# The second group's two w_out products as seven block products, and its w_in product ordered by block column

## The chip, the cores and the metric

The kernel runs on one core of one Trainium2 chip. Its time is that of one execution on the device, in microseconds (us); it is compared as the median of several executions.

## The reference

An attention layer that mixes heads before and after the softmax is followed by two feed-forward layers:

```python
scores = scale * np.matmul(q, k.transpose(0, 1, 3, 2))           # 4 batches, 12 heads, 448 x 448, head size 64
scores = np.einsum('bhij,hg->bgij', scores, w_pre)
attn = softmax(scores)                                            # over the last axis
attn = np.einsum('bhij,hg->bgij', attn, w_post)
x = np.matmul(attn, v)                                            # as 1792 tokens x 768
h = x @ w_in;  g = np.maximum(h, 0) ** 2;  x = g @ w_out          # first layer: w_in 768 x 2048, w_out 2048 x 768
h = x @ w_in2; g = h * np.clip(h + 3, 0, 6) / 6; y = g @ w_out2   # second layer, same sizes
```

## The kernel before

The four batches are done in two groups of two. Each group runs attention for its 896 tokens and then the two feed-forward layers. Every float32 matrix product there is made of three products of parts: each operand is split into a high part and a low part (what the high part leaves), and high by high, low by high and high by low are summed in PSUM. TensorE sees 128x128 weight blocks against 448 token columns, so one instruction is a 128x128x448 matmul.

*Attention* (class Attention). A group has 90 tiles of ten query rows by twelve heads. `slot(i)` writes one step of a pipeline over tiles: `fetch` (a transfer t<-s, six tiles ahead, on SyncE's queue, called SP here), `premix` (TensorE, three tiles ahead), `top`, `soft`, `scale` (GpSimd makes w2s for the next tile), `postmix` and `keep`. Fetches of q, k and v, and the score and value products, are placed in slots by `plan`. The tiles t have eight buffers, so SP may run ahead until a buffer is missing. The order on each engine is the order in the program.

*Feed-forward* (class Mlps). The weights come in units of 128 rows by 768 columns: 16 units for w_in (kind "h", one per 128 hidden columns) and 16 for w_out (kind "p") in each layer. The first group reads each as float64 words, converts them and writes a float32 copy to DRAM (`kept`); the second group reads the copies. `split_high` and `split_low` make wh on ScalarE and wl on VectorE or GpSimd, one unit ahead. One unit is 36 matmuls: 3 products x 6 blocks x 2 batches. `hidden` and `project` issue them; `act` and `split_g` make the activation and its two parts.

*The second group* already has one product in another form: the second layer's w_in product (kind "s"). Two units of w_in (256 hidden columns) and the token matrix are cut into 2x2 blocks, and four block results come from seven block products instead of eight (the Winograd form of Strassen's scheme). `prepare`, during the first layer's w_in units, loads two kept units, makes four sums of their blocks on VectorE and writes them to DRAM (`sums`); `finish_mixed` makes the token side from the first layer's output while it leaves PSUM; `product` issues 9 matmuls for one block product; `combine`, `step` and `relu` add the results and form the activation. There are 56 such products, 504 matmuls in place of 576. The last product (w_out of the second layer) is direct.

SP's queue takes all loads and stores in program order, with the waits in front of each; results leave on ScalarE's queue.

Of the kernel before, what the change touches and what calls it, by code (L numbers as in the profile page):

```python
# [44 lines left out]
LATE = 10  # L45
# [20 lines left out]
def attention_mlp_kernel(ctx: ExitStack, tc, qT, kT, v, w_pre, w_post, mask, w1_in, w1_out, w2_in, w2_out, outT):  # L66
# [56 lines left out]
    class Attention:  # L123
# [317 lines left out]
        def run(self, ap, behind):  # L441
# [21 lines left out]
    kept, sums = {}, {}  # L463
    HW = DM // 2

    class Mlps:
        def __init__(self, gi, att):
            self.gi, self.att = gi, att
            self.last = gi > 0 and gi == B // NB - 1
            self.units, at = [], 0  # L470
            for which, (w_in, w_out) in enumerate(((w1_in, w1_out), (w2_in, w2_out))):
                if self.last and which == 1:
                    self.base = at
                    self.prods = [(p, 2 * j + i) for j in range(NF // 4) for p, i in PRODUCTS]
                    self.units += [("s", which, n, None) for n in range(len(self.prods) // 2)]
                else:
                    self.units += [("h", which, n, (w_in[n], at + n)) for n in range(NF)]
                at += NF
                self.units += [("p", which, n, (w_out[n // NU, n % NU], at + n)) for n in range(DG * NU)]
                at += DG * NU  # L480
            self.W = w1_in.shape[-1]
            self.mp, self.own, self.u, self.r, self.gates = None, {}, {}, {}, 0
            self.gate = self.opened = None
            self.lows, self.loads = set(), set()
            self.arena, self.ready, self.late, self.scaled = None, {}, [], set()
# [5 lines left out]
        def wr(self, n):  # L491
            if n in self.own:
                return self.own[n]
            at = 2 * 2 * self.W + self.W * (n % 3)
            return self.arena[:, at:at + self.W]

        def load(self, n):
            if n >= len(self.units) or n in self.loads:
                return
            self.loads.add(n)  # L500
            kind, _, m, src = self.units[n]
            if self.last and n >= NF:
                self.own[n] = self.mp.tile([P, self.W], F32, tag="wr", name=f"wr{n}", bufs=3)
            elif self.arena is None:
                self.arena = sh.tile([P, 7 * self.W], F32, tag="e1", name=f"arena{self.gi}")
            if self.gi == 0:
                nc.sync.dma_start(out=self.raw(n).bitcast(I64), in_=src[0])
            elif kind != "s":
                nc.sync.dma_start(out=self.wr(n), in_=kept[src[1]])
            else:  # L510
                for i in range(2):
                    p, pair = self.prods[2 * m + i]
                    a = self.base + 2 * pair
                    if p in SUMS:
                        of = sums[pair][:, SUMS[p] * HW:(SUMS[p] + 1) * HW]
                    else:
                        of = kept[a + (p == 4)][:, (p > 1) * HW:(1 + (p > 1)) * HW]
                    nc.sync.dma_start(out=self.wr(n)[:, i * HW:(i + 1) * HW], in_=of)

# [26 lines left out]

        def split(self, n):
            self.split_high(n)
            self.split_low(n)

        def split_high(self, n):
            if n >= len(self.units) or n in self.ready:
                return
            if self.last and n >= self.base and (n - self.base) % 3 == 1:
                both = self.mp.tile([P, 2, self.W], F32R, tag="pr", name=f"wb{n}", bufs=1)
                wh, wl = both[:, 0, :], both[:, 1, :]
            else:
                wh = sh.tile([P, self.W], F32R, tag="wh", name=f"wh{self.gi}_{n}", bufs=2)
                wl = sh.tile([P, self.W], F32R, tag="wl", name=f"wl{self.gi}_{n}", bufs=2)
            nc.scalar.activation(wh, self.wr(n), AF.Copy)  # L560
            self.ready[n] = wh, wl

        def split_low(self, n):
            if n >= len(self.units) or n in self.lows:
                return
            self.lows.add(n)
            wh, wl = self.ready[n]
            eng = nc.vector if self.gi == 0 or self.last and n >= self.base else nc.gpsimd
            eng.tensor_tensor(out=wl, in0=self.wr(n), in1=f(wh), op=ALU.subtract)  # L569
# [34 lines left out]
        def hidden(self, which, fc, e, wh, wl):  # L604
            cols = slice(e * S, (e + 1) * S)
            hp = self.bank("bm", f"ps_h{self.gi}_{which}_{fc}_{e}")
# [39 lines left out]
        def bank(self, tag, name):  # L646
            if self.last:
                return self.mb.tile([128, 512], F32, tag="pb", name=name, bufs=8)
            return bank(tag, name)

        def prepare(self, n):

            if not self.last or n >= NF:
                return
            m, odd = n // 2, n % 2
            if not odd:
                self.pr = self.mp.tile([P, 4, HW], F32, tag="pr", name=f"pr{m}", bufs=1)
                for i in range(2):
                    nc.sync.dma_start(
                        out=self.pr[:, 2 * i:2 * i + 2, :].rearrange("p c f -> p (c f)"), in_=kept[self.base + 2 * m + i])  # L660
                return
            a11, a12, a21, a22 = (self.pr[:, i, :] for i in range(4))
            nc.vector.tensor_tensor(out=a22, in0=a21, in1=a22, op=ALU.add)
            nc.vector.tensor_tensor(out=a21, in0=a11, in1=a21, op=ALU.subtract)
            nc.vector.tensor_tensor(out=a11, in0=a22, in1=a11, op=ALU.subtract)
            nc.vector.tensor_tensor(out=a12, in0=a12, in1=a11, op=ALU.subtract)
            sums[m] = dr.tile([P, 4 * HW], F32, name=f"sums{m}")
            nc.sync.dma_start(out=sums[m], in_=self.pr.rearrange("p c f -> p (c f)"))

        def part(self, hi, lo, src):  # L670
            nc.scalar.activation(hi, src, AF.Copy)
            nc.gpsimd.tensor_tensor(out=lo, in0=src, in1=f(hi), op=ALU.subtract)

        def finish_mixed(self, dg, e, acc):

            def held(tag, name, bufs=2):
                return (sh if bufs > 1 else self.mp).tile([P, S], F32, tag=tag, name=name, bufs=bufs)
            if dg == 0 and e == 0:
                self.b1, self.b2, self.b3 = (
                    sh.tile([P, 4, DB, S], F32R, tag=tag, name=f"b{k}") for k, tag in ((1, "x1"), (2, "x2"), (3, "e1")))  # L680
                self.t1 = [held(("w0", "w0", "w1")[d], f"t1_{d}") for d in range(DB)]
                self.t3 = [held(("w1", "kr", "kr")[d], f"t3_{d}") for d in range(DB)]
            if dg == 1 and e == 0:
                self.t4 = [held(("gh9_0", "gh9_1", "gl9_0")[d], f"t4_{d}", 1) for d in range(DB)]
                self.b4 = [[self.mp.tile([P, S], F32R, tag=f"gh{10 + (j * DB + d) // 2}_{(j * DB + d) % 2}",
                                         name=f"b4_{j}_{d}", bufs=1) for d in range(DB)] for j in range(2)]
            for d in range(DB):
                a = acc[d, e][:, :S]
                b1, b2, b3 = (t[:, :, d, :] for t in (self.b1, self.b2, self.b3))
                t1, t3 = self.t1[d], self.t3[d]  # L690
                if dg == 0 and e == 0:
                    nc.scalar.activation(b1[:, 0], a, AF.Copy)
                    nc.vector.tensor_tensor(out=b1[:, 1], in0=a, in1=f(b1[:, 0]), op=ALU.subtract)
                    nc.scalar.activation(t1, a, AF.Copy)
                elif dg == 0:
                    nc.vector.tensor_tensor(out=t1, in0=a, in1=t1, op=ALU.subtract)
                    nc.scalar.activation(t3, a, AF.Copy)
                    self.part(b2[:, 0], b2[:, 1], t1)
                elif e == 0:
                    nc.scalar.activation(b1[:, 2], a, AF.Copy)  # L700
# [279 lines left out]
```

## Time and profile before

| | |
|---|---|
| median of 3 runs (lowest to highest) | 1394.34 us (1394.15 to 1394.59) |
| the profiled execution: its own time, its span | 1396.4 us, 1394.6 us |
| TensorE matmul (PE) busy | 1373.3 us, 98% of the span |
| VectorE (DVE) busy | 788.9 us, 57% |
| ScalarE (ACT) busy | 568.2 us, 41% |
| GpSimd (POOL) busy | 349.1 us, 25% |
| 16 DMA engines, mean | 129 GB/s |

The profile is of one execution. "Busy" counts an engine's compute instructions, not its waits. A matmul's duration in it (some 365 ns) is the time through the engine's pipeline; the distance from one to the next is read from long chains. Queries of the trace cut the span by stage, list an engine's instructions in order, or follow the chain of work that ended last.

### The profile page before, as it was taken

To read this page: it belongs to the slowest core of one execution; us is meant where nothing else is said; L and a number is where in the kernel's file an instruction comes from. 1 tells how busy PE (TensorE), PEld (TensorE's weight loads), DVE (VectorE), ACT (ScalarE), POOL (GpSimd) and SP (SyncE) were. 2 spreads that over 40 slices of the span, in tenths; PEclk is the share of its full clock that TensorE was granted. 3 is DMA by queue.
4 is the path that set the end of the run, shared out by engine and by line. 5 is a ranking of instruction groups with operands and counts; after the bars stand their busy time and mean duration, and the time that the engine had idled before them with its cause. 6 is when DMAs were issued, how large, how long until landed. Compare 5 with 4: busy or idle time off the path is not lost.

```text
span 1394.6 us, 22295 instructions
## 1 busy us (share of the span) xinstructions
PE 1373.3 (98%) x8428; PEld 1183.0 (85%) x8428; DVE 788.9 (57%) x1441; ACT 568.2 (41%) x1060; POOL 349.1 (25%) x411
## 2 busy tenths in 40 slices
PE   7999999999999999999999999999999999999999
PEld 3677778899989899998987777779999998999998
DVE  4677667877655587765546776763431105875110
ACT  3454434555322355534234544444342214654021
POOL 0222122434200033310012221245663224423000
PEclk9999999999999999999999999999999999999999
DMA  5453533555555455566644535324453112332121
GB/s 164 120 149 97 136 101 102 180 170 163 165 156 162 144 162 170 161 200 187 201 136 129 146 84 147 102 89 137 145 182 99 50 57 69 114 114 91 57 85 40
DMA packets 77585, 179.98 MB, mean 129 GB/s; under 512 B 7846, under 2 KB 51622, under 8 KB 77478
## 3 DMA queue, kind: packets, MB, share of 16 engines
q1 hardware_dynamic: 74021, 173.06, 41.8%
q10 hardware_dynamic: 3456, 5.51, 1.1%
q8 instruction: 66, 1.08, 0.3%
q14 instruction: 42, 0.34, 0.1%
HBM read 103.04 MB, written 36.96 MB: 100 GB/s over the span
## 4 chain that ended last, share of the span: by engine, by line
PE 93%; DVE 3%; DMA 1%; ACT 1%; issue 1%; POOL 0%; SPq 0%; ACTq 0%; POOLq 0%; DVEq 0%
PE ps_h L610 25%; PE ps_a L624 22%; PE ps_o L275 11%; PE ps_m L227 9%; PE ps_w L730 7%; PE bx L624 5%; PE bs L624 5%; PE bx L302 3%; PE bs L302 2%; PE bs L200 2%; PE bx L200 2%; DMA t<-s 1%; PE ps_s L315 1%; DVE wl L569 0%; PE ps_s L200 0%
## 5 line engine op out<-in xcount | busy, mean ns | idle before, releaser
L275 PEld LDWEIGHTS ps_o<-w2s,p 120*112 120x112 f32 (+1 forms) x1440 | 170.5, 178 | 71.4 <-issue 57.1
L244 ACT ACTIVATE p<-ps_m,mx 120x448 f32<-120x448 f32 x180 | 114.0, 633 | 188.5 <-PE ps_o L275 87.5
L275 PE MATMUL ps_o<-w2s,p 120*112 120x120 f32 (+1 forms) x1440 | 182.0, 270 | 1.9 <-POOL w2s L264 1.8
L227 PE MATMUL ps_m<-t,w1f 120*120 120x448 f32 x360 | 167.8, 548 | 7.5 <-DMA t<-s 7.4
L264 POOL TENSOR_SCALAR w2s<-w2f,rz 120x120 f32<-120x120 f32 x180 | 65.8, 365 | 360.8 <-DVE rz L256 317.2
L610 PE MATMUL ps_h<-xh,wh 128*128 128x448 f32 x384 | 140.5, 366 | 1.5 <-DVE xr L310 1.5
L610 PE MATMUL ps_h<-xh,wl 128*128 128x448 f32 x384 | 140.3, 365 | 0.2 <-DVE wl L569 0.2
L610 PE MATMUL ps_h<-xl,wh 128*128 128x448 f32 x384 | 139.6, 364 | 0.1
L290 DVE COPY a<-ps_o 112x480 f32<-112x480 f32 (+1 forms) x176 | 115.0, 653 | 32.0 <-PE ps_o L275 22.2
L602 POOL TENSOR_TENSOR gl<-g,gh 128x448 fp32r<-128x448 f32 x60 | 77.2, 1287 | 219.6 <-ACT gh L601 165.9
L236 DVE TENSOR_REDUCE mx<-ps_m 120x1 f32<-120x448 f32 x180 | 111.5, 620 | 25.2 <-PE ps_m L227 22.1
L569 DVE TENSOR_TENSOR wl<-arena,wh 128x768 fp32r<-128x768 f32 x64 | 62.8, 981 | 104.9 <-ACT wh L560 104.0
L624 PE MATMUL ps_a<-gh,wh 128*128 128x448 f32 x320 | 118.2, 369 | 0.0
L560 ACT ACTIVATE wh<-arena 128x768 fp32r<-128x768 f32 x80 | 67.0, 838 | 123.4 <-PE bs L624 120.4
L624 PE MATMUL ps_a<-gh,wl 128*128 128x448 f32 x320 | 116.5, 364 | 0.0
L560 ACT ACTIVATE wh<-wr 128x768 fp32r<-128x768 f32 x45 | 37.9, 842 | 137.0 <-PE ps_a L624 124.3
L569 DVE TENSOR_TENSOR wl<-wr,wh 128x768 fp32r<-128x768 f32 x29 | 29.7, 1025 | 96.3 <-ACT wh L560 96.3
L587 ACT ACTIVATE r<-ps_h 128x448 f32<-128x448 f32 x64 | 34.8, 543 | 111.4 <-PE ps_h L610 111.4
L610 PEld LDWEIGHTS ps_h<-xh,wh 128*128 128x128 f32 x384 | 72.1, 188 | 7.4 <-issue 1.9
L610 PEld LDWEIGHTS ps_h<-xl,wh 128*128 128x128 f32 x384 | 72.2, 188 | 6.7 <-POOL xl L579 0.9
L599 DVE CAST gh<-g 128x448 fp32r<-128x448 f32 x64 | 39.6, 618 | 66.4 <-ACT g L588 66.4
L610 PEld LDWEIGHTS ps_h<-xh,wl 128*128 128x128 f32 x384 | 72.0, 188 | 5.6 <-DVE wl L569 0.5
(167 smaller groups left out, 3020.7 us busy)
## 6 DMA issues: line engine op xcount, KB each, us to landing
arena<-in_dram SPq DMA_DIRECT2D x64, 768.0 KB
t<-s SPq DMA_DIRECT2D x176, 210.0 KB
keep<-arena SPq DMA_DIRECT2D x64, 384.0 KB
wr<-keep SPq DMA_DIRECT2D x32, 384.0 KB
arena<-keep SPq DMA_DIRECT2D x16, 384.0 KB
pr<-keep SPq DMA_DIRECT2D x16, 384.0 KB
sums<-pr SPq DMA_DIRECT2D x8, 768.0 KB
wr<-sums SPq DMA_DIRECT2D x32, 192.0 KB
```

Of the source, the lines that this page charges most:

```text
L227: nc.tensor.matmul(m[:rows, :S], lhsT=w1f.rearrange("p i g -> p (i g)")[:rows, :rows], rhs=self.live.pop(("t", i))[:rows], start=True, sto ...
L236: nc.vector.reduce_max(mx[:rows], m[:rows, :S], axis=AX.X, negate=True)
L244: nc.scalar.activation(pt[:rows], m[:rows, :S], AF.Exp, bias=mx[:rows], accum_out=z[:rows])
L275: nc.tensor.matmul(o[:JP, q * G * ni:(q + 1) * G * ni], lhsT=pt[:rows, q * JP:(q + 1) * JP], rhs=w2s[:rows, :G * ni], start=True, stop=True)
L290: nc.vector.tensor_copy(dst, src)
L302: nc.tensor.matmul(xo[e * D:(e + 1) * D, k * n:(k + 1) * n], lhsT=self.v[:, q, g, :], rhs=self.aa[c][:, q, g, :n], start=(q == 0), stop=(q ...
L560: nc.scalar.activation(wh, self.wr(n), AF.Copy)
L569: eng.tensor_tensor(out=wl, in0=self.wr(n), in1=f(wh), op=ALU.subtract)
L602: nc.gpsimd.tensor_tensor(out=gl, in0=g, in1=f(gh), op=ALU.subtract)
L610: nc.tensor.matmul(hp[:, :S], lhsT=lw[:, c * P:(c + 1) * P], rhs=rw[:, c, cols], start=(k == 0), stop=(k == 3 * KC - 1))
L624: nc.tensor.matmul(acc[d, e][:, :S], lhsT=lw[:, wc], rhs=rw[fc, e], start=(fc == 0 and k == 0), stop=(fc == NF - 1 and k == 2))
L730: nc.tensor.matmul(to[:, :S], lhsT=lw[:, wc], rhs=rw, start=(d == 0 and j == 0), stop=(d == DB - 1 and j == 2))
```

## The change

In the second group all three products after the first w_in product now take the seven-product form, by a new class `Blocks`:

- The first layer's w_in stays direct ("plain": 16 units of 36 matmuls).
- Both w_out products are cut in 2x2 blocks over hidden rows and output columns, the tokens by batch: seven products, each of 4 units of 18 matmuls ("out": 28 units per layer). Token-side sums are made in place on VectorE in `operands`, five units ahead (AHEAD), with high parts on ScalarE and low parts on VectorE, one in four on GpSimd. `close_product` puts the additions of results, and the next layer's operands (`operand`), in a list `tasks`, from which `work` issues three or five per unit.
- The second layer's w_in goes by product column ("in": 28 units of two products, `IN_STEPS`), no longer pair by pair.
- Weights are split three units ahead, loaded up to five ahead. For block products whose weights are plain blocks of w_out (first layer) and w_in (second layer), the low part isn't computed: the first group writes it to DRAM (`store_low`, 28 more transfers), and the second group loads it in `split_high`.
- The block sums of the weights are 24 jobs now (8 for each of three weight matrices), each a load of 768 KB, four additions of 128x384 and a store of 768 KB. Ten run during the second group's attention (`beside`: the additions on GpSimd, one in every second slot; per eight slots one store and one load on SP), fourteen in the plain units (`under`: VectorE, one per unit). In the kernel before, eight ran in sixteen units.

Core of the diff (the removed functions are those quoted above as kind "s"):

```diff
-PRODUCTS = (
-    (1, 0), (1, 1), (2, 0), (2, 1), (6, 0), (7, 0), (5, 0), (4, 0), (3, 0), (6, 1), (7, 1), (5, 1), (4, 1), (3, 1),
-)
+IN_STEPS = (((1, 0),), ((5, 0),), ((6, 0), (1, 1)), ((7, 0), (5, 1)), ((3, 0), (6, 1)), ((2, 0), (7, 1)), ((4, 0), (3, 1)), ((2, 1), (4, 1)))
+BESIDE, AHEAD = 10, 5
+OUT_PRODUCTS = (1, 5, 2, 6, 7, 3, 4)
...
             for i in range(self.n + 1):
                 self.slot(i)
+                if beside:
+                    beside(ap, i)
...
+        def store_low(self, n, wl):
+
+            if B <= NB or n < NF or n >= UNITS + NF:
+                return
+            if n < UNITS:
+                if (n - NF) // (NU // 2) == DG:
+                    return
+                cols = slice(0, self.W)
+            else:
+                cols = slice((n - UNITS) % 2 * HW, self.W)
+            low_kept[n] = dr.tile([P, self.W], F32, name=f"low{n}")
+            nc.sync.dma_start(out=low_kept[n][:, cols], in_=f(wl)[:, cols])
...
+        def beside(self, ap, i):
+
+            j, o = (i - 2) // 8, (i - 2) % 8
+            todo = self.beside_todo
+            if i < 2:
+                return
+            if o == 0 and 2 <= j < len(todo) + 2:
+                prepare(*todo[j - 2], 2)
+            if o == 1 and j < len(todo):
+                prepare(*todo[j], 0, [ap.tile([P, 2, HW], F32, tag=f"pr{r}", name=f"pr{r}_{j}", bufs=3) for r in range(2)])
+            if o % 2 == 1 and 1 <= j <= len(todo):
+                prepare(*todo[j - 1], 1, eng=nc.gpsimd, ks=(o // 2,))
+
+        def under(self, n):
+
+            todo = self.under_todo
+            if n == 0:
+                self.pr = sh.tile([P, 3, 2, 2, HW], F32, tag="e1", name="pr")
+            if 2 <= n < len(todo) + 2:
+                prepare(*todo[n - 2], 2)
+            if n < len(todo):
+                prepare(*todo[n], 0, [self.pr[:, n % 3, r] for r in range(2)])
+            if 1 <= n <= len(todo):
+                prepare(*todo[n - 1], 1, eng=nc.vector)
...
+        def operands(self, n):
...
+                of = {5: (b, a), 6: (d, a), 7: (d, b), 4: (c, a)}.get(p)
+                if of:
+                    nc.vector.tensor_tensor(out=src, in0=of[0], in1=of[1], op=ALU.subtract)
...
+            for src, hi, _ in made:
+                nc.scalar.activation(hi, src, AF.Copy)
+
+            def low(q):
+                src, hi, lo = made[q]
+                eng = nc.gpsimd if (u * UF + q) % 4 == 1 else nc.vector
+                eng.tensor_tensor(out=lo, in0=src, in1=f(hi), op=ALU.subtract)
+            return [lambda q=q: low(q) for q in range(UF)]
...
+        def out_unit(self, which, p, u, wh, wl):
+            if u == 0:
+                self.acc = [self.bank(f"ps_y{which}_{p}_{d}") for d in range(DB)]
+            for d in range(DB):
+                for q in range(UF):
+                    wc = slice(q * HW + d * P, q * HW + (d + 1) * P)
+                    bh, bl = self.ops[p, u * UF + q]
+                    for j, (lw, rw) in enumerate(((wh, bh), (wl, bh), (wh, bl))):
+                        nc.tensor.matmul(
+                            self.acc[d][:, :S], lhsT=lw[:, wc], rhs=rw, start=(u == 0 and q == 0 and j == 0),
+                            stop=(u == NU // 2 - 1 and q == UF - 1 and j == 2))
...
+            for n, (kind, which, what) in enumerate(self.units):
+                for k in (3, 4, 5):
+                    self.load(n + k)
+                wh, wl = self.ready.pop(n)
...
+                self.out_unit(which, p, u, wh, wl)
+                self.split_high(n + 3)
+                lows = self.operands(n + AHEAD)
+                self.split_low(n + 3)
+                for low in lows:
+                    low()
+                self.work(5 if not lows else 3)
+                if u == NU // 2 - 1:
+                    self.close_product(which, p)
```

## Rows read from the trace of the kernel before

**Rows 1.** The page's busy times: engine, share of the span, instructions.
```profile
PE 1373.3 (98%) x8428; PEld 1183.0 (85%) x8428; DVE 788.9 (57%) x1441; ACT 568.2 (41%) x1060; POOL 349.1 (25%) x411
```

**Rows 2.** Busy times by stretch of the second group, in us.
```profile
core 0: us, PE busy (x) PEld busy (x) DVE busy (x) ACT busy (x) POOL busy (x), PEclk, DMA share, GB/s
720.00:926.00 206.00, 205.66 (x1793) 154.02 (x1792) 144.52 (x384) 98.29 (x234) 47.12 (x108) 1.00 0.45 123
...
937.30:1054.00 116.70, 116.69 (x577) 108.39 (x578) 49.86 (x64) 48.03 (x81) 69.33 (x49) 1.00 0.45 152
1054.00:1170.70 116.70, 116.70 (x577) 107.88 (x576) 10.06 (x18) 23.61 (x36) 32.83 (x20) 1.00 0.23 71
1170.70:1180.00 9.30, 8.32 (x41) 7.24 (x40) 7.37 (x13) 7.58 (x15) 9.17 (x8) 1.00 0.01 2
```

**Rows 3.** The chain that ended last: start us, us, what.
```profile
937.31 116.73 PE ps_h L610 x576
...
1179.58 95.04 PE ps_w L730 x467
1274.62 116.53 PE ps_a L624 x576
```

**Rows 4.** Groups of instructions, shapes apart: count, busy us, mean ns, idle before.
```profile
L569 DVE TENSOR_TENSOR wl<-wr,wh 128x768 fp32r<-128x768 f32 x29 | 29.7, 1025 | 96.3 <-ACT wh L560 96.3
L569 POOL TENSOR_TENSOR wl<-wr,wh 128x768 fp32r<-128x768 f32 x16 | 29.5, 1843 | 70.5 <-ACT wh L560 70.5
L672 POOL TENSOR_TENSOR gls<-gs,ghs 128x448 fp32r<-128x448 f32 x20 | 27.1, 1359 | 37.2 <-ACT ghs L671 37.2
L664 DVE TENSOR_TENSOR pr<-pr 128x384 f32<-128x384 f32 x8 | 17.6, 2194 | 0.3
L663 DVE TENSOR_TENSOR pr<-pr 128x384 f32<-128x384 f32 x8 | 4.4, 551 | 0.0
```

**Rows 5.** VectorE in order, middle of the "s" units: start us, us, instruction.
```profile
1211.28 0.62 DVE L737 TENSOR_TENSOR u<-ps_w,u 128x448 f32<-128x448 f32 x1
1211.81 0.95 DVE L569 TENSOR_TENSOR wl<-wr,wh 128x768 fp32r<-128x768 f32 x1
1212.68 0.62 DVE L737 TENSOR_TENSOR gs<-ps_w,u 128x448 f32<-128x448 f32 x1
```

**Rows 6.** DMA, 937 to 1054 us in 40 slices of 2.9 us: busy tenths, rate.
```profile
DMA  9100087700877008770098700977009770097600
GB/s 337 65 3 0 6 269 244 294 0 0 269 254 289 0 0 269 251 287 0 0 273 259 276 4 0 277 249 280 0 0 306 239 267 6 0 295 258 253 0 6
```

**Rows 7.** SP's own waits, 720 to 926 us: total, times, longest.
```profile
SPq L221 <- PE ps_m L227: 31.3, 33, 2.3
```

**Rows 8.** SP, GpSimd and TensorE in order: tile 25's fetch, w2s of slot 18, two premixes.
```profile
757.65 1.53 SPq L221 DMA_DIRECT2D t<-s  x1
...
763.35 0.36 POOL L264 TENSOR_SCALAR w2s<-w2f,rz 120x120 f32<-120x120 f32 x1 [0.28 <-DVE rz L256]
...
773.29 0.92 PE L227 MATMUL ps_m<-t,w1f 120*120 120x448 f32 x2
...
774.87 0.92 PE L227 MATMUL ps_m<-t,w1f 120*120 120x448 f32 x2
```

**Rows 9.** SP in order, first group's attention: two loads of v, 672 KB each.
```profile
22.10 1.78 SPq L163 DMA_DIRECT2D v<-in_dram  x1
...
25.54 0.49 SPq L163 DMA_DIRECT2D v<-in_dram  x1
```

**Rows 10.** The chain that ended last, right behind them.
```profile
26.14 10.74 DMA t<-s
```

**Rows 11.** First group, w_out units: SP's load, and VectorE's next-but-one split.
```profile
379.28 0.33 SPq L507 DMA_DIRECT2D arena<-in_dram  x1
...
389.80 0.96 DVE L569 TENSOR_TENSOR wl<-arena,wh 128x768 fp32r<-128x768 f32 x1 [3.27 <-ACT wh L560]
```

More of the change, by code (lines that the diff above doesn't have):

```diff
@@ L439, in slot, with run @@
                             fn(*args)
-        def run(self, ap, behind):
+        def run(self, ap, behind, beside=None):
             self.ap = ap
@@ L460, in closing, with prepare @@
             return [lambda v=v: self.values(c, v) for v in range(NV)]
-    kept, sums = {}, {}
+    kept, low_kept, sums = {}, {}, {}
     HW = DM // 2
+    UNITS = NF + DG * NU
+    held = {}
+    def prepare(kind, which, i, stage, tiles=None, eng=None, ks=range(4)):
+        key = kind, which, i
+        if stage == 0:
+            held[key] = tiles
+            at = which * UNITS
+            for j in range(2):
+                if kind == "in":
+                    nc.sync.dma_start(out=tiles[j], in_=kept[at + 2 * i + j].rearrange("p (c f) -> p c f", c=2))
+                    continue
+                u, cols = i // 2, slice(i % 2 * HW, (i % 2 + 1) * HW)
+                for k in range(2):
+                    nc.sync.dma_start(out=tiles[j][:, k, :], in_=kept[at + NF + j * NU + k * NU // 2 + u][:, cols])
+        elif stage == 1:
+            a11, a12, a21, a22 = (t[:, k, :] for t in held[key] for k in range(2))
+            for k in ks:
+                out, one, other, op = (
+                    (a22, a21, a22, ALU.add), (a21, a11, a21, ALU.subtract), (a11, a22, a11, ALU.subtract),
+                    (a12, a12, a11, ALU.subtract))[k]
+                eng.tensor_tensor(out=out, in0=one, in1=other, op=op)
+        else:
+            to = sums[key] = dr.tile([P, 4 * HW], F32, name=f"sums_{kind}{which}_{i}")
+            for j, t in enumerate(held.pop(key)):
+                nc.sync.dma_start(out=to[:, 2 * j * HW:2 * (j + 1) * HW].rearrange("p (c f) -> p c f", c=2), in_=t)
     class Mlps:
@@ L468, in __init__ @@
             self.gi, self.att = gi, att
-            self.last = gi > 0 and gi == B // NB - 1
-            self.units, at = [], 0
+            self.units = []
             for which, (w_in, w_out) in enumerate(((w1_in, w1_out), (w2_in, w2_out))):
[L472 to L480, printed above, removed]
+                self.units += [("h", which, n, w_in[n]) for n in range(NF)]
+                self.units += [("p", which, n, w_out[n // NU, n % NU]) for n in range(DG * NU)]
             self.W = w1_in.shape[-1]
-            self.mp, self.own, self.u, self.r, self.gates = None, {}, {}, {}, 0
-            self.gate = self.opened = None
-            self.lows, self.loads = set(), set()
             self.arena, self.ready, self.late, self.scaled = None, {}, [], set()
@@ L497, in load @@
         def load(self, n):
-            if n >= len(self.units) or n in self.loads:
+            if n >= len(self.units):
                 return
[L500 to L504, printed above, removed]
+            if self.arena is None:
                 self.arena = sh.tile([P, 7 * self.W], F32, tag="e1", name=f"arena{self.gi}")
             if self.gi == 0:
-                nc.sync.dma_start(out=self.raw(n).bitcast(I64), in_=src[0])
-            elif kind != "s":
-                nc.sync.dma_start(out=self.wr(n), in_=kept[src[1]])
-            else:
[L511 to L518, printed above, removed]
+                nc.sync.dma_start(out=self.raw(n).bitcast(I64), in_=self.units[n][3])
+            else:
+                nc.sync.dma_start(out=self.wr(n), in_=kept[n])
         def convert(self, n, part=None):
@@ L868, in run @@
                 alone = not behind and which == 1 and dg == DG - 1
-                if u == 0 and self.last:
-                    acc = {(d, e): self.bank("pb", f"ps_a{self.gi}_{which}_{dg}_{d}_{e}")
-                           for e in range(NB) for d in range(DB)}
-                elif u == 0:
+                if u == 0:
                     acc = {}
@@ L882, in run @@
                                 acc[d, e] = bank("bm", nm) if alone else bs[:, e, :]
-                if m == 0 and which == 0 and not self.last:
+                if m == 0 and which == 0:
                     self.yh = sh.tile([P, KC, T], F32R, tag="x1", name=f"yh{self.gi}")
@@ L888, in run @@
                     self.project(u, e, wh, wl, acc)
[L889 to L893 removed]
+                    if ends:
                         self.finish(which, dg, e, range(DB), acc)
[L895 removed]
+                if which == 0 and m == DG * NU - 1:
                     self.xh, self.xl = self.yh, self.yl
```

464 lines of the change are left out of this document (270 added, 194 removed).

## The prediction, made before the changed kernel was run

> **What bounds the kernel now.** I read the page's busy times first: TensorE is busy 98% of the span, VectorE 57% [rows 1]. An average says little about one stage, so I cut the second group by stage: attention has 205.66 us of matmul in 206, the w_in and w_out units of the first layer leave nothing idle, and only the passage into the block products (1170.7 to 1180) shows 0.98 us without a matmul [rows 2]. Then the chain that ended last: behind attention it is TensorE alone, without a break longer than that passage [rows 3]. The reader should see that here the number of matmuls is the time, as long as operands come in time. The clock is granted at 1.00, the 2.4 GHz level, in all these stretches [rows 2].
>
> **One matmul.** 576 matmuls took 116.73 us in the first chain row and 116.53 us in the last, so 202.7 and 202.3 ns each; the block products took 203.5 (95.04 us for 467) [rows 3]. I use 202.5 ns for all forms, since each has the same 128x128 weights and 448 columns.
>
> **What is removed.** Before: 576 + 576 + 504 + 576 = 2232 matmuls, from 937.31 to 1391.14 (the last row's end), 453.83 us; 2232 x 0.2025 = 452.0, so some 1.8 us in it isn't matmul [rows 3]. After: 576 + 3 x 504 = 2088, or 422.8 us. The 144 matmuls are 29.2 us; with the 1.8 us, 31.0 us is the most that this stretch can give. The tail (copy and transfer of the last result) keeps its form and I cost it at nothing new.
>
> **VectorE in the w_out block products.** This is the engine that gets the work. A unit lasts 18 x 0.2025 = 3.645 us, 28 units 102.1 us. In the first layer's 28 units I count 16 weight splits of 768 columns (the other 12 come from DRAM), 32 token differences, 42 low parts and 48 additions or operand steps of 448 columns. Taken one by one (1.025 us [rows 4] and 0.62 us [rows 5]) that is 16.4 + 122 x 0.62 = 92.0 us. Back to back they follow each other sooner: 0.53 us after a 448-column one and 0.87 us after a split [rows 5], which gives 13.9 + 64.7 = 78.6 us. On top come meetings with GpSimd, which makes 14 low parts of 1.36 us each: a 128x384 addition took 2.19 us where GpSimd worked beside it and its like 0.55 us alone [rows 4], so up to 1.64 us a meeting, 23 us for 14. Low end 78.6, high end 115.0, against 102.1. In the second layer all 28 splits are VectorE's and the other steps fall to 95: 74.8 to 110.6 us. I take the back-to-back figure with all meetings, 101.6 and 97.8 us, as VectorE's queue will be dense: just within TensorE's time, with crowded units (up to 4.6 us of work in 3.65) evened out by operands made five and weights three units ahead (18.2 and 10.9 us). Loss taken: nothing; ends 0 and 12.9 + 8.5 = 21.4 us. The "in" units are lighter: 88 additions and gates, 16 us of splits and some 30 leftover steps, 88 x 0.62 + 16.4 + 18.6 = 89.6 us in 102.1.
>
> In words of the Trainium skill (SBUF — State Buffer, Who interferes with whom), a VectorE instruction with two SBUF inputs and a GpSimd one that reads SBUF exclude each other for the whole instruction. The pair of 2.19 and 0.55 us agrees [rows 4], and by that rule all 28 GpSimd low parts would block VectorE for 1.36 us each, 38 us over both stages, less than the 46 us that I counted in the high end.
>
> **Transfers in the plain units.** Each 7.29 us unit now moves 384 KB of weights, 768 KB in and 768 KB out: 1.97 MB, 270 GB/s. Before, with half as many jobs, transfers ran in bursts at 239 to 306 GB/s with two of five slices empty [rows 6]. So the engines would be full nearly all the time. At 240 GB/s a unit needs 8.2 us, and after 14 units the queue is 13 us late. Weights are asked five units ahead (36 us), so the plain units hide this; it would show in the first "out" units, where a lead of three units is 10.9 us. I take the middle of the measured rates, so nothing; ends 0 and 13 us.
>
> The Trainium skill (DMA: Bandwidth & Descriptors, Specifications) puts a core's HBM limit at some 358 GB/s; by it 270 GB/s would leave a quarter free and the high end would be nothing too. No 2.9 us slice in the steady part of that stage reached it [rows 6].
>
> **Attention of the second group.** Ten jobs ride there. GpSimd: forty additions at half of 1.843 us [rows 4], 0.92 us each, in every second slot. A slot is 1.58 us (premix to premix [rows 8]) and w2s takes 0.36, so it fits where no q is split. SP is the delicate part. Today it runs ahead until a tile buffer is missing (33 waits for premix [rows 7]): tile 25's fetch was issued at 757.65, 15.6 us before its premix at 773.29 [rows 8]. Now SP must wait, once in eight slots, for the job's last addition. For slot 18 that is w2s at 763.35 + 0.36 + 0.92 = 764.6 us. Behind this wait stand a 768 KB store, tile 25's fetch, a 768 KB load, then tile 26's fetch. They have 8.7 and 10.3 us to land. A fetch in the first group landed 10.74 us after issue [rows 10] with two 672 KB transfers queued in the 4 us before it [rows 9]; at 270 GB/s the store and load alone are 5.8 us. So tile 26 may come 0 to 3 us late, and in the last tiles, where all slots are short, both. About half of the eight waits that have both store and load fall ahead of a value stretch (some 4.7 us longer slots) and cost nothing; I take four at 1.25 us: 5 us. Ends: 0, and 8 x 5.8 = 46 us if nothing is hidden.
>
> **First group.** `store_low` adds 384 KB to a unit's 1152 KB, 1.57 MB in 7.29 us or 216 GB/s, below the rates above. It also holds wl longer: issued right behind the load at 379.28, while the buffer is next written at 389.80 [rows 11], 10.5 us, against 5.8 us for 1.57 MB at 270 GB/s. Cost: nothing; if that cover went (late by 1 us in each of 28), 28 us.
>
> **Passages.** Plain to "out", "out" to "in" and back need operands and PSUM banks whose last reader is deep in `tasks`. The old passage cost about 1 us of matmul [rows 2]; three new ones, 0 to 6 us: I take 2.
>
> **Sum.** -31.0 + 5 + 2 = -24.0 us. The profiled execution's own time was 1396.4 us (span 1394.6 and 1.8 around it), so 1372.4; the median of the runs stands 2.1 us below that execution, so 1370.3 us.
>
> **Rivals.** (A) VectorE becomes the bound in the "out" units. For it: a dense queue and GpSimd beside it; against: the back-to-back rows. It adds up to 21.4 us: 1371 to 1392. (B) The jobs in attention hold up the fetches. For it: SP's lead of 15 us goes at each wait, and row 10; against: the long slots. Each of eight waits would have to cost 3.6 us beyond cover before the gain of 29 us is gone; that is the point from which the kernel becomes slower, and at 5.8 us each it would be 1394.3 - 29 + 46 = 1411 us. (C) The plain units fill the DMA engines and the first "out" weights come late: up to 13 us, 1383. (D) Everything is hidden: 1394.3 - 31.0 = 1363.3.
>
> **How the numbers follow.** My forecast, losses between 0 and 14 us (1363 to 1377): 0.60, D at its end. A: 0.10, C: 0.10. B short of the turning point (1377 to 1391): 0.12; B near or beyond it: 0.08. Of A, C and the first part of B (0.32) some six tenths, 0.19, lie between 1377 and 1385; with the forecast's 0.60 that is 0.79, so the range ends at 1385. It begins at 1363, as nothing in the sum goes lower. Runs differ by 0.03%, and 0.2% (2.8 us) is about what can be told from no change. Faster by more than that 0.90, within it 0.04, slower 0.06.
>
> **What would show it.** Right: 2088 matmuls in the second group at 202 to 203 ns; no idle TensorE behind attention longer than 2 us; plain units with a DMA share near the top of its scale and unchanged length (116.7 us); attention longer by some 5 us, with premix waiting on t<-s. Wrong: wl or low parts of VectorE as releasers of TensorE within "out" units (A); premix waits of several us in each eighth slot (B); wh or wl waiting on transfers at the first "out" units (C); a matmul distance above 0.205 us; or a first group that lengthens in its w_out and second w_in units.

## The result, and the profile after

The changed kernel takes 1373.57 us (median of 4 runs, 1373.51 to 1374.02) where the kernel before, on the same chip, takes 1394.24 (1393.42 to 1394.59): ratio 0.9853, 95% interval 0.9836 to 0.987. That is 20.7 us faster, 3.3 us less than the 24.0 forecast. The profiled execution took 1373.51 us, its span is 1371.6.

The page's busy times, to be read against [rows 1]:
```profile
PE 1345.7 (98%) x8284; PEld 1156.8 (84%) x8284; DVE 917.8 (67%) x1668; ACT 626.2 (46%) x1167; POOL 290.7 (21%) x372
```
TensorE has 144 matmuls fewer, VectorE 129 us more. Busy times by stretch of the second group (attention, plain, "out", "in", "out"), as in [rows 2]:
```profile
core 0: us, PE busy (x) PEld busy (x) DVE busy (x) ACT busy (x) POOL busy (x), PEclk, DMA share, GB/s
717.48:944.23 226.75, 216.67 (x1915) 162.86 (x1914) 150.53 (x395) 102.19 (x242) 89.90 (x153) 0.99 0.61 182
944.23:1060.96 116.73, 116.73 (x577) 108.46 (x578) 53.39 (x80) 53.24 (x91) 4.99 (x4) 1.00 0.77 260
1060.96:1163.50 102.54, 102.54 (x506) 94.68 (x505) 78.89 (x119) 56.44 (x97) 17.99 (x12) 1.00 0.48 148
1163.50:1265.38 101.88, 101.88 (x505) 94.63 (x505) 76.75 (x131) 57.14 (x91) 3.07 (x2) 1.00 0.47 146
1265.38:1367.90 102.52, 102.50 (x504) 94.33 (x503) 80.05 (x120) 48.51 (x82) 33.12 (x12) 1.00 0.35 112
```
The chain that ended last, behind attention, as in [rows 3]:
```profile
944.23 116.73 PE ps_h L612 x576
1060.96 102.53 PE ps_y L956 x504
1163.50 101.88 PE ps_w L860 x504
1265.38 102.52 PE ps_y L956 x504
```
The four rows join without a gap: 423.67 us for 2088 matmuls, 202.9 ns each, against 453.83 us before. Feed-forward of the second group gave 30.16 us. Attention took most of the difference to the forecast: from the first group's feed-forward to the second's it was 250.41 to 937.31 before, 686.90 us, and is now 246.91 to 944.23, 697.32 us, 10.4 us more. The end behind the last matmul grew by 0.24 us. Against the two profiled spans (1394.6 and 1371.6, 23.0 us) this leaves 3.5 us at the start: the first group's feed-forward began at 250.41 us before and at 246.91 here, with the same code ahead of it. In the profiles of the runs below that start lies between 246.2 and 248.9, and the execution profiled before was itself 2.1 us above its kernel's median, so the 3.5 us are taken as a difference between executions, not as an effect of the change. That is not shown: the kernel before has one profile.

What TensorE waited for in the second group's attention (total, times, longest):
```profile
PE ps_m L227 <- DMA t<-s: 3.8, 3, 1.7
PE ps_m L227 <- ACT p L244: 2.7, 1, 2.7
PE ps_o L275 <- POOL w2s L264: 1.5, 4, 0.6
```
And SP's own waits in the same stretch, beside [rows 7]:
```profile
SPq L494 <- POOL pr L490: 33.3, 8, 9.4
SPq L221 <- PE ps_o L275: 16.1, 22, 1.6
SPq L221 <- PE ps_m L227: 15.0, 22, 1.5
SPq L494 <- POOL w2s L264: 6.1, 1, 6.1
...
SPq L221 <- DVE s L205: 4.2, 2, 3.7
```
The fetches' waits (L221) behind premix have halved, from 31.3 to 15.0 us, while those put down to postmix (L275) are 16.1 for 12.9. Clearer is another row: before, from 720 to 926 us, SP had run so far ahead that it waited for the scores themselves (s, L205), and now it hardly does:
```profile
SPq L221 <- DVE s L205: 36.2, 7, 8.0
```
So SP no longer runs as far ahead. In their place stand nine waits of the stores (L494) for GpSimd, 39.4 us in all and up to 9.4: SP gets there long before the job's last addition. SP in order around the first of them (start us, us, instruction), then the chain there, then ScalarE's and TensorE's rows behind it and the stretch that follows:
```profile
761.23 1.34 SPq L494 DMA_DIRECT2D sums_out<-pr  x2
762.67 1.21 SPq L221 DMA_DIRECT2D t<-s  x1
763.97 0.45 SPq L172 DMA_DIRECT2D qr<-in_dram  x1
764.47 2.66 SPq L483 DMA_DIRECT2D pr<-keep  x4
767.23 0.82 SPq L221 DMA_DIRECT2D t<-s  x1
768.09 0.49 SPq L144 DMA_DIRECT2D kr<-in_dram  x1
```
```profile
770.02 3.43 DMA t<-s
...
773.46 0.71 ACT p L244 x2
```
```profile
772.98 0.58 ACT L158 ACTIVATE khl<-kr 128x448 fp32r<-128x448 f32 x1 [3.04 <-DMA kr<-in_dram]
774.22 1.78 PE L227 MATMUL ps_m<-t,w1f 120*120 120x448 f32 x2 [2.67 <-ACT p L244]
```
```profile
774.20:777.60 3.40, 3.38 (x11) 2.47 (x12) 3.29 (x10) 1.45 (x4) 2.29 (x4) 0.52 0.66 181
```
The store, a fetch, the 768 KB load and the next fetch follow each other within 7 us. The chain names a fetch t<-s from 770.02 on, but ScalarE's row shows which transfer was late: raw keys (kr, L144), issued at 768.09 behind the load. ScalarE waited 3.04 us to split them (khl), the softmax p stood behind that split in its queue, and premix waited 2.67 us for the softmax. Before, the same keys were issued at 764.40 for a split at 773.31, and no split waited. The last row has the columns of the stretches above: TensorE's granted clock (PEclk) was 1.00 up to the wait and is 0.52, close to the 1.2 GHz level, in the 3.4 us after it; premix and postmix took 1.78 and 1.81 us there, against 0.92 and 0.98 just before, together 1.7 us more. It is the kind of place that the prediction described, but with another transfer, and at a higher price. At two later places premix itself waits on t<-s, as forecast (rows of the chain):
```profile
851.42 5.59 DMA t<-s
909.85 4.79 DMA t<-s
```

### The profile page after: what moved, and what is told of

The parts are those of the page before. It is cut to its first block, busy times and chain, and to the rows that moved or that the text cites. A ratio compares the mean times of both kernels' runs of the same rounds, so it can differ in the third digit from the quotient of the medians.

```text
span 1371.6 us, 22671 instructions
## 1 busy us (share of the span) xinstructions
PE 1345.7 (98%) x8284; PEld 1156.8 (84%) x8284; DVE 917.8 (67%) x1668; ACT 626.2 (46%) x1167; POOL 290.7 (21%) x372
## 4 chain that ended last, share of the span: by engine, by line
PE 92%; DVE 2%; DMA 2%; SPq 1%; ACT 1%; issue 1%; POOL 0%; POOLq 0%; ACTq 0%; DVEq 0%
PE ps_h L612 25%; PE ps_y L956 15%; PE ps_o L275 10%; PE ps_m L227 9%; PE ps_w L860 7%; PE bx L626 6%; PE bs L626 6%; PE ps_a L626 5%; PE bx L302 3%; PE bs L302 2%; PE bs L200 2%; PE bx L200 2%; DMA t<-s 2%; SPq L221 1%; PE ps_s L315 1%
## 5 line engine op out<-in xcount | busy, mean ns | idle before, releaser
L275 PEld LDWEIGHTS ps_o<-w2s,p 120*112 120x112 f32 (+1 forms) x1440 | 170.6, 178 | 72.2 <-issue 56.4
L275 PE MATMUL ps_o<-w2s,p 120*112 120x120 f32 (+1 forms) x1440 | 182.3, 270 | 2.6 <-POOL w2s L264 2.5
L956 PE MATMUL ps_y<-o,wx 128*128 128x448 f32 x504 | 106.8, 365 | 0.0
L612 PE MATMUL ps_h<-xh,wl 128*128 128x448 f32 x288 | 105.3, 366 | 0.1
L956 PEld LDWEIGHTS ps_y<-o,wx 128*128 128x128 f32 x504 | 94.6, 188 | 7.7
L956 PE MATMUL ps_y<-o,wh 128*128 128x448 f32 x336 | 100.4, 366 | 0.0
L945 POOL TENSOR_TENSOR o<-gi,o 128x448 fp32r<-128x448 f32 x14 | 36.2, 2590 | 175.3 <-DVE gi L891 108.3
L612 PE MATMUL ps_h<-yh,wh 128*128 128x448 f32 x192 | 70.2, 366 | 0.0
L612 PE MATMUL ps_h<-yh,wl 128*128 128x448 f32 x192 | 70.1, 365 | 0.0
L612 PE MATMUL ps_h<-yl,wh 128*128 128x448 f32 x192 | 69.7, 363 | 0.0
L227 PEld LDWEIGHTS ps_m<-t,w1f 120*120 120x120 f32 x360 | 52.4, 185 | 18.6 <-ACT p L244 6.7
L956 PEld LDWEIGHTS ps_y<-o,wh 128*128 128x128 f32 x336 | 63.1, 188 | 5.4
```

The source lines that it names most:

```text
L227: nc.tensor.matmul(m[:rows, :S], lhsT=w1f.rearrange("p i g -> p (i g)")[:rows, :rows], rhs=self.live.pop(("t", i))[:rows], start=True, sto ...
L275: nc.tensor.matmul(o[:JP, q * G * ni:(q + 1) * G * ni], lhsT=pt[:rows, q * JP:(q + 1) * JP], rhs=w2s[:rows, :G * ni], start=True, stop=True)
L612: nc.tensor.matmul(hp[:, :S], lhsT=lw[:, c * P:(c + 1) * P], rhs=rw[:, c, cols], start=(k == 0), stop=(k == 3 * KC - 1))
L956: nc.tensor.matmul(self.acc[d][:, :S], lhsT=lw[:, wc], rhs=rw, start=(u == 0 and q == 0 and j == 0), stop=(u == NU // 2 - 1 and q == UF - ...
```

## The experiments

All runs were timed beside the kernel before, whose medians were 1393.33, 1393.81 and 1395.03 us in the three sets. Two lengths are read from the chain of each profile: A, from the first group's feed-forward to the second's (the same code but for the jobs, 686.90 us before), and F, the second group's feed-forward.

| run | median us | ratio to before, 95% interval | A | F |
|---|---|---|---|---|
| the change | 1373.57 | 0.9853 (0.9836 to 0.987) | 697.32 | 423.67 |
| e1_no_jobs_beside | 1363.35 | 0.9784 (0.977 to 0.9799) | 686.88 | 423.67 |
| e2_late_store | 1366.73 | 0.981 (0.9796 to 0.9825) | 689.24 | 423.67 |
| e3_wait_few_bytes | 1371.27 | 0.984 (0.9825 to 0.9855) | 691.50 | 423.66 |
| b1_period_seven | 1365.53 | 0.9796 (0.9781 to 0.9811) | 686.89 | 423.67 |
| e4_lows_vector | 1375.72 | 0.988 (0.9864 to 0.9897) | 698.85 | 423.65 |
| e5_no_low_kept | 1374.04 | 0.9863 (0.9843 to 0.9883) | 697.83 | 423.66 |
| e6_split_two_ahead | 1418.39 | 1.0174 (1.0149 to 1.0199) | not read | 467.61 |
| e8_two_ahead_adds_after | 1375.03 | 0.9856 (0.9831 to 0.988) | 697.49 | 425.00 |
| e7_operands_two_ahead | 1378.9 | 0.9894 (0.9876 to 0.9913) | 696.77 | 428.45 |
| e9_two_ahead_lows_vector | 1373.49 | 0.9839 (0.9817 to 0.9861) | 699.15 | 423.67 |

Six of the profiles with an A have the change's own attention code; it runs from 696.8 to 699.2 us in them, so a difference of 2 us there says nothing. Part of that spread is the clock: at the first place above ScalarE waits 2.1 to 3.1 us for the raw keys in all six, but only in three (the change, e4, e9) did the granted clock fall behind it, to between 0.52 and 0.55 for some 3.5 us.

**Where attention lost 10 us.** Theory 1: SP's wait takes its lead, and the store and load that stand behind it then delay a fetch that has none left. Rivals: the bytes alone, or the wait alone.

```diff
# e1_no_jobs_beside
-            self.beside_todo, self.under_todo = todo[:BESIDE], todo[BESIDE:]
+            self.beside_todo, self.under_todo = [], todo[BESIDE:]
# e2_late_store (and bufs=4 for the job's tiles)
-            if o == 0 and 2 <= j < len(todo) + 2:
-                prepare(*todo[j - 2], 2)
+            for job in range(len(todo)):
+                if i == min(8 * job + 25, self.att.n):
+                    prepare(*todo[job], 2)
# e3_wait_few_bytes (few = 8 of 384 columns in the jobs' loads and stores)
-                    nc.sync.dma_start(out=tiles[j][:, k, :], in_=kept[...][:, cols])
+                    nc.sync.dma_start(out=tiles[j][:, k, :few], in_=kept[...][:, cols][:, :few])
```


> Leaves out the ten jobs that ride beside attention (their loads, additions and stores); the seven products that would read their sums read kept weight blocks instead, in transfers of the same size. All theories: the second group's attention falls from 226.8 to some 216.5 us, as before the change, so some 1363.3 us. If it stays above 220, the longer attention has another cause than the jobs.

> The same jobs and the same bytes, but each store is issued seven slots later (four buffers instead of three), so that SP no longer waits for the job's last GpSimd addition. Theory 1 (the wait takes SP's lead, and the store and load then stand ahead of a fetch that is already late): attention 217 to 219.5 us, 1364 to 1366.5 us. Rival (the bytes alone: 1.5 MB for each job on the DMA engines, whenever they are issued): attention stays at 225 to 227, 1372 to 1374 us.

> SP's wait for the job's last addition stays, with all forty GpSimd additions, but each of the jobs' transfers moves 8 columns instead of 384 (the sums aren't made; the products read kept blocks as in the run without jobs). Theory 1: the wait alone leaves the fetches some 10 us, so nearly all is hidden: attention 217 to 219, 1364 to 1366 us, the rest being GpSimd's additions at the end (1.2 us). Rival, the wait alone: attention 225 to 227. Rival, the bytes alone: 217 to 219 too, so this run tells only the wait alone from the others.

The first and the third leave out the sums of the ten jobs; the products read kept weight blocks in their place. In the third the tiles are zeroed first, by six VectorE instructions. Without jobs attention is exactly as before (686.88 against 686.90), so all 10.4 us are the jobs'. With the stores issued later, and a fourth buffer for that, same jobs and bytes, 8.1 of them come back; no split waits for raw keys there. The median, 1366.73 us, is 0.2 above the range expected, the attention stretch (218.67 us) within it. Of the stores' waits one long one is left, at the last stores, for which no later slot is left:
```profile
SPq L494 <- POOL pr L490: 13.2, 1, 13.2
```
So the bytes alone are not it. The third run was a miss for theory 1 as written, which gave it 217 to 219 us for the attention stretch: it is 220.77 (719.63 to 940.40), and 4.6 us remain against the run without jobs. SP's waits for GpSimd are as long as in the change (39.6 us in nine), and at the first place the raw keys come late even where the jobs move hardly any bytes, so that TensorE waits for the softmax behind their split:
```profile
SPq L494 <- POOL pb L490: 30.7, 6, 9.2
```
```profile
773.85 0.58 ACT L158 ACTIVATE khl<-kr 128x448 fp32r<-128x448 f32 x1 [1.96 <-DMA kr<-in_dram]
```
```profile
PE ps_m L227 <- ACT p L244: 2.4, 2, 1.6
```
Cut at the value products (bx L302 in the chain), each part of attention can be laid beside the run without jobs:

| from value product to value product | 1 to 2 | 4 to 5 | 6 to 7 | 7 to 8 |
|---|---|---|---|---|
| no jobs (e1) | 27.28 | 27.27 | 22.17 | 15.12 |
| the change | 31.56 | 29.82 | 24.32 | 16.37 |
| bytes, hardly a wait (e2) | 27.28 | 27.58 | 22.98 | 16.39 |
| wait, hardly any bytes (e3) | 29.37 | 27.27 | 23.47 | 16.39 |
| period seven (b1) | 27.28 | 27.27 | 22.18 | 15.12 |

The other parts differ by at most 0.2 us. In the first three columns the wait with hardly any bytes costs 3.4 us, the bytes with hardly a wait 1.1 and both together 9.0: more than the sum, so theory 1 holds for some 4.5 us of it, and the wait by itself for 3.4. These are single profiles: in the six with the change's attention code the three columns lose between 7.7 and 10.7 us, so the excess over the sum lies between 3.2 and 6.2. About 1.7 of the 9.0 is the lower clock of the first column. And 0.8 of the 1.1 is hardly the bytes': between the value products 6 and 7 of e2 the chain goes through GpSimd, an addition (L490, 908.48 us), a token split (L581, 909.43) and then w2s (910.57). The last column, 1.25 us, is the same in all three runs with additions on GpSimd up to the end. There the chain goes through GpSimd (row of the changed kernel's chain):
```profile
927.94 0.36 POOL w2s L264
928.31 0.74 POOL pr L490
...
929.23 1.05 POOL xl L581
...
930.34 0.37 POOL w2s L264
```
An addition and a token split stand in front of the w2s that postmix needs. The version that follows from both:

```diff
# b1_period_seven
+            for job in range(len(todo)):
+                o = i - 7 * job
+                if o == 21:
+                    prepare(*todo[job], 2)
+                if o == 3:
+                    prepare(*todo[job], 0, [ap.tile(..., bufs=4) for r in range(2)])
+                if o in (8, 10, 12, 14):
+                    prepare(*todo[job], 1, eng=nc.gpsimd, ks=(o // 2 - 4,))
```


> The ten jobs in attention every seven slots instead of eight, four buffers, each store seven slots after the job's last addition and three before the next load; the last addition is in slot 77, so none is left in attention's tail. Theory 1 (wait and bytes together cost 9 us, GpSimd's additions 1.25 us in the tail): attention 216.5 to 218 us, the tail behind the last value stretch back from 18.3 to 17.1, in all 1363.5 to 1366 us. Rival (bytes alone, now denser): attention 220 us or more, 1367 us or more.

Every part of attention is back at the length without jobs, with the same ten jobs and the same bytes. The wait rows of the stretch show why: the stores' waits for GpSimd are down from 39.4 us to 6.0, the longest from 9.4 to 1.6, and ScalarE's wait for raw keys from 3.0 to 0.3. (It differs from the change in the period, the stores' slots, the buffers and the last slot at once; which of them would do alone is not tested, beyond the later stores of e2.)
```profile
SPq L494 <- POOL w2s L264: 6.0, 5, 1.6
```
At 1365.53 us it has the lowest median of the versions that leave nothing out; its interval (0.9781 to 0.9811) lies wholly below that of the change, though it overlaps that of e2 (0.9796 to 0.9825).

**Is VectorE near its bound in the "out" units?**

```diff
# e4_lows_vector
-                eng = nc.gpsimd if (u * UF + q) % 4 == 1 else nc.vector
+                eng = nc.vector
# e5_no_low_kept: store_low returns at once
-            if B <= NB or n < NF or n >= UNITS + NF:
+            if True:
```


> The 28 token-side low parts that GpSimd makes in the two w_out stages go to VectorE. By the prediction's sum VectorE gets 14 x 0.53 = 7.4 us more in each stage and loses its meetings with GpSimd; it has room, so 1373.5 within 0.5 us. By rival A (VectorE near its bound): some us slower, with TensorE waiting on low parts in the w_out units.

> The first group keeps no low parts; the second group's first layer makes all its weight low parts on VectorE (12 more of 768 columns in its w_out stage). By the prediction's sum the 28 transfers of the first group cost nothing, and 12 x 0.87 = 10.4 us more for VectorE fit beside 78.9 us busy in 102.5: no stage changes, 1373.5 to 1376 us (the attention of two profiles with the same attention code differs by 1.6 us). If the transfers do cost something, the first group's 236.4 us from its first w_out unit to the end of its second w_in units shortens; if VectorE is near its bound, the second group's first w_out stage grows beyond 102.5.

F did not move in either. e4's median, 1375.72 us, is outside the 1373.0 to 1374.0 expected. Its profiled span is 2.4 us longer than the change's: 1.5 us lie in attention, 0.8 at the start, both ahead of its edit, so in that execution nothing of it belongs to the edit. Its two "out" stages:
```profile
1063.31:1165.84 102.53, 102.53 (x505) 94.63 (x505) 77.41 (x131) 56.49 (x97) 0.00 (x0) 1.00 0.49 148
1267.72:1370.24 102.52, 102.51 (x504) 94.31 (x503) 80.17 (x131) 48.18 (x81) 0.00 (x0) 1.00 0.35 111
```
VectorE has 12 and 11 instructions more than in the change, and is busy 1.5 us less in the first stage and 0.1 more in the second. What GpSimd took off it, it gave back in longer instructions (groups from the first "out" stage on, where gp belongs to the first layer and gi to the second; the change, then e4):
```profile
L945 DVE TENSOR_TENSOR o<-gi,o 128x448 fp32r<-128x448 f32 x42 | 26.7, 662 | 0.1
...
L936 DVE TENSOR_TENSOR gp<-gp,gp 128x448 f32<-128x448 f32 x30 | 22.1, 776 | 0.0
...
L945 POOL TENSOR_TENSOR o<-gi,o 128x448 fp32r<-128x448 f32 x14 | 36.2, 2590 | 175.3 <-DVE gi L891 108.3 <-ACT o L940 67.0
```
```profile
L945 DVE TENSOR_TENSOR o<-gi,o 128x448 fp32r<-128x448 f32 x56 | 32.3, 619 | 0.1
...
L936 DVE TENSOR_TENSOR gp<-gp,gp 128x448 f32<-128x448 f32 x30 | 17.3, 619 | 0.0
```
In e5 VectorE is busy 87.6 us of the first "out" stage, against 78.9, and TensorE still never waits. The first group's stretch from its first w_out unit to the end of its second w_in units was 236.35 us before the change and 236.36 with it, so its 28 added transfers cost nothing; that the low parts are kept saves nothing either, while VectorE has the room.

**How much of the leads is needed?**

```diff
# e6_split_two_ahead (in all units, and one unit fewer split ahead of the first)
-                            self.split_high(n + 3)
-                            self.split_low(n + 3)
+                            self.split_high(n + 2)
+                            self.split_low(n + 2)
# e8_two_ahead_adds_after: e6, and in the plain units
-                    self.under(n)          # loads, stores and VectorE's additions
+                    self.under(n)          # loads and stores
                     ...
                             self.split_low(n + 2)
+                            self.under_add(n)
# e7_operands_two_ahead; e9_two_ahead_lows_vector: the same with e4's edit
-BESIDE, AHEAD = 10, 5
+BESIDE, AHEAD = 10, 2
```


> Weights are split two units ahead instead of three. By the prediction three units (10.9 us) even out units with up to 4.6 us of VectorE work in 3.65. If two (7.3 us) are enough, the second group's MLP stays at 423.7 us; if VectorE's queue is behind by more than that at crowded units, TensorE waits for wl in the block products and the stretch grows by up to 10 us.

> Weights split two units ahead, as in the run that took 1418 us, but in the plain units VectorE's four additions of a job are issued behind the weight split instead of ahead of it. Theory (queue order: VectorE waits in its queue for the job's load, and the weight split stands behind that wait): TensorE no longer waits for wl and wx in the plain units, the second group's MLP falls from 467.6 us to 424 to 432, the kernel to 1374 to 1383 us. Rival (transfer rate: with 270 GB/s asked for, the weights themselves come late, and only a third unit covers that): the plain units stay above 145 us and the kernel above 1400.

Two units are not enough, and the place was in neither theory of e6: of the 43.9 us, 42.4 fall in the plain units, not in the block products. VectorE's wait in the plain units (total, times, longest), first in the change, then in e6, then in e8:
```profile
DVE pr L490 <- DMA pr<-keep: 23.9, 10, 7.1
```
```profile
DVE pr L490 <- DMA pr<-keep: 102.3, 14, 9.9
```
```profile
DVE pr L490 <- DMA pr<-keep: 7.2, 10, 2.4
```
One turn of it in e6, VectorE in order:
```profile
1066.28 2.33 DVE L490 TENSOR_TENSOR pr<-pr 128x384 f32<-128x384 f32 x4 [9.18 <-DMA pr<-keep]
1068.53 0.95 DVE L791 TENSOR_TENSOR wx<-wr,wx 128x768 fp32r<-128x768 f32 x1
```
The four additions of a job wait 9.18 us for its load, and the weight split, whose operands have long been there, stands behind them. TensorE waits for wx and wl (30.2 us in ten waits in these units). It comes round: SP's next load of weights waits for the buffer that this split reads, goes out as the split ends, and the next job's load stands behind it in SP's queue, at 1070.83 us.
```profile
1069.51 0.32 SPq L764 DMA_DIRECT2D wr<-keep  x1
```
The other 12 us come with the clock: among these waits the plain units' granted clock is 0.91 in the mean, between its levels of 1.2 and 2.4 GHz, instead of 1.00, and their 576 matmuls are busy 128.7 us instead of 116.7. In e8 the splits stand ahead of the additions and two units are enough there: 116.73 us for the plain units, F 425.00; the last 1.3 us are low parts from DRAM that come late in the "in" units and what follows (TensorE's longest wait for wl<-low: 0.8 us). So queue order is shown as the cause, and the transfer rate is refuted: the bytes are the same.

> Operands of the w_out block products are made two units ahead instead of five (7.3 us instead of 18.2). If VectorE has slack in every unit (78.9 us busy of 102.5), the MLP stretch stays within 1 us of 423.7; if its work comes in lumps that need the five units, TensorE waits for low parts at the first units of a product: 424.7 to 434 us.

> Operands two units ahead, as in the run that took 1379 us, with all token-side low parts on VectorE. If the 3.2 us wait of that run came from GpSimd being slow at its low part while VectorE's queue is dense, it goes: MLP stretch 423.7 to 424.5 us instead of 428.5, and 1373.5 to 1376 us in all. If it came from too short a lead for VectorE's work, it stays or grows: 428 us or more.

With operands two units ahead TensorE has one wait in the block products, and it is for GpSimd (GpSimd's and TensorE's rows):
```profile
1347.83 9.84 POOL L945 TENSOR_TENSOR o<-gi,o 128x448 fp32r<-128x448 f32 x2 [6.86 <-ACT o L940]
...
1356.62 0.50 PEld L956 LDWEIGHTS ps_y<-o,wh 128*128 128x128 f32 x2 [3.61 <-POOL o L945]
```
One low part took 8.74 us there; the shortest of its kind took 1.14. With all low parts on VectorE the wait is gone and F is 423.67: it was GpSimd, not VectorE's load. In the change a low part near the same place is as slow, 8.76 us from 1344.72 on, and TensorE has no wait there: five units of lead hide it.

## Why the prediction came out as it did

- **Matmuls.** Right: 31.0 us taken, 30.16 measured; the difference is the distance between matmuls, 202.9 ns for the 202.5 used. The passages, taken at 2 us, cost nothing.
- **VectorE in the "out" units.** The loss of nothing was right, its price too high: 101.6 and 97.8 us of work were costed, 78.9 and 80.05 are busy. Two terms were too large. The first stage has 119 VectorE instructions, not the 138 counted, which is some 10 us at the prediction's 0.53. And the meetings: by e4 each costs VectorE (78.89 + 12 x 0.62 - 77.41) / 12 = 0.74 us in the first stage (0.65 with 0.53 us for 0.62), not 1.64, while GpSimd's low parts grow, to 2590 ns in the mean in the second layer instead of 1359 [rows 4]. Rival A had no ground in the change: TensorE waits for nothing in these units. The Trainium skill's rule (SBUF — State Buffer, Who interferes with whom) that such a pair excludes each other for the whole instruction agrees with these rows in direction, as either engine's instructions are longer beside the other's. The 38 us that the prediction worked out from it for VectorE's side were not there.
- **Plain units.** Unchanged length was right (116.73 us at 260 GB/s); the DMA share, forecast near the top of its scale, was 0.77. The cover that the prediction named, weights asked five units ahead, did not hold alone: e6 keeps it and loses 42 us. What held was the third unit of split lead, since VectorE's queue waits for the jobs' loads ahead of the splits. It missed that queue when it listed what a late transfer stops, and the queue order behind that cost is shown by e8.
- **Attention.** The step that was mis-sized: "I take four at 1.25 us: 5 us" measured 10.4. The mechanism, SP's lead lost at its waits and late transfers behind them, was right. Three places lost 4.28, 2.55 and 2.15 us. At the last two premix waited on t<-s, as written. At the first it was another transfer of the same queue, the raw keys, whose fetch the program places one slot ahead of their split: the prediction listed only the tiles behind SP's wait. About 1.7 us of this place is the clock granted after TensorE's wait, a price that the sum has no term for. The prediction priced only transfers behind a lost lead; the wait alone, with next to no bytes, already costs 3.4 us. And 1.25 us came from GpSimd's additions in the last slots, which it put at nothing on the ground that they fit between two w2s: the token splits on GpSimd in those slots weren't counted.
- **First group.** Nothing, as taken.
- **From the profile to the median.** On the profiled executions 23.0 us of span were gained, on the medians 20.7, since the execution profiled before was 2.1 us above the median and the one after 0.06 below it. By medians the miss of 3.3 us is the attention's 5.4 us too little, the matmuls' 0.8 and the end's 0.2, less the 2 us of the passages, which cost nothing, and some 1.2 us of an earlier start (3.5 in the profiles less those 2.1). That the time came so close to the forecast is in part luck: the passages, taken too high, and the start, which nobody forecast, made up for more than half of what attention lost beyond its 5 us.

## What to carry to other kernels

Before a store is put on a queue that others use for loads, look at what it waits for: give it enough steps after its producer, and another buffer, so that it never holds the queue; here that recovered 8 of 10 us, and a schedule that also ends the additions before the busy last slots the rest. List every transfer on such a queue with its lead, not only the frequent ones: here the place with the late raw keys, fetched one slot ahead of their use, cost between 2.3 and 4.6 us in the six profiles. The chain's name for a late transfer is inferred; look at what the engine in front of the wait itself waited for. An in-order engine that waits for a transfer delays everything queued behind it, so work whose inputs are already there goes ahead of work that waits for a load. When a stage has no idle time, test its leads one at a time: the one that mattered here (42 us) was not the one that the forecast relied on.

## What the runs showed of the hardware

A GpSimd subtraction of 128x448 beside a dense VectorE queue took up to 8.76 us in the change, where its shortest is 1.15; lending VectorE's low parts to it saved VectorE 0.1 us in one stage and cost it 1.5 in the other. Behind a wait of TensorE of 2.67 us its granted clock was 0.52 for 3.4 us in the change; behind one of 1.89 us at the same place of e5 it stayed at 1.00. The transfer rate in slices of 2.9 us reached 394 GB/s in the plain units, against at most 306 in [rows 6] (337 in its first slice):
```profile
GB/s 0 62 293 323 266 34 331 307 358 325 303 383 356 319 314 309 182 394 154 311 347 151 384 165 308 341 161 383 154 328 330 6 83 393 287 328 372 292 153 121
```
The Trainium skill's 358 GB/s for a core's HBM (DMA: Bandwidth & Descriptors, Specifications) is passed in single slices, which its page Perfetto Trace Analysis (Roofline) allows to a core that runs alone; the mean over the stage, 260, stays below it.
